# Expert matmuls in four column strips during attention, and the last 64 keys on the same tiles with zeros in V

## The chip, the cores and the metric

The kernel runs on one core of one Trainium2 chip. The core has a matrix engine (TensorE, PE in the profile, with its weight loads shown apart as PEld), a vector engine (VectorE, DVE), a scalar engine (ScalarE, ACT), a general engine (GpSimd, POOL), which here only starts loads, and SyncE (SP), which starts stores. Sixteen DMA engines move data between the chip's main memory and the on-chip memory. The metric is the time of one execution on the device, in microseconds (us); lower is better.

## What is computed

Attention of 8 batches, 12 heads, 448 tokens and 64 numbers a head, and behind it a feed-forward layer ("experts" below) on its 3,584 rows of 768:

```python
def _attn_ref(q, k, v):
    scale = 1.0 / np.sqrt(q.shape[-1])
    scores = scale * np.matmul(q, k.transpose(0, 1, 3, 2))
    scores = scores - np.max(scores, axis=-1, keepdims=True)
    attn = np.exp(scores)
    attn = attn / (np.sum(attn, axis=-1, keepdims=True) + 1e-09)
    return np.matmul(attn, v)

def _moe_ref(x, w_in, w_out):          # w_in 768 x 2048, w_out 2048 x 768
    h = x @ w_in
    g = h * (1.0 / (1.0 + np.exp(-h)))
    return g @ w_out
...
x = attn_out.transpose(0, 2, 1, 3).reshape(B * S, H * D)
return _moe_ref(x=x, **moe_kwargs)
```

## The kernel before

*Units.* Heads are taken four at a time, so a batch has three head groups. A unit is one head group of one batch; batch 0 is cut in two pieces of 224 tokens, so that it has six units of 224 and the other batches have three of 448, 27 units in all. The 448 keys of a group lie in four chunks (`c` = 0 to 3). In the first four groups ("lone") these chunks have 128, 128, 96 and 96 keys. From there on two groups go together, "low" and "high": each fills three chunks of 128 and has 64 keys left; the low group's are put in partitions 0 to 63 of the fourth chunk, the high group's in 64 to 127, so that both share one tile of exponentials, `E[(ns[0], 3)]`.

*Attention on PE.* Scores (L327) run on row tiles: a head's 64 numbers are folded to 32 partitions and two steps, so four matmuls on 32x128 tiles run together, one for each head. ACT takes the exponential (L364) into `E`. The row sums (`attend_sums`, L406) and the product with V (`attend_mm`, L390) run on column tiles: 128 keys by 32 columns, four heads together. For a pair the fourth chunk's product uses eight 64x32 tiles, four heads of each of the two groups. DVE inverts the sums and multiplies (L443 to L473), which leaves the rows of x, transposed, in `xT`.

*Experts on PE.* `ffn1` (L487) makes one 128-column piece of h from six matmuls on the full 128x128 array; ACT takes tanh and DVE the gate into `G`. The output product is done for four blocks at a time with seven products in place of eight (`product`, L685; `combine_g` and `combine_w` make the sums for it on DVE); two row blocks are done plainly (`plain`, L699). The last two batches use a seven-product form for h too (`pair_product`, L622), which runs when attention is over.

*Weights of a tile.* A matmul instruction on PE always stands behind its own weight load, so each matmul is two instructions in PE's order.

*The order.* It is written out beforehand: `Order` keeps a clock for each engine, every piece of work is an `Op` with an assumed cost, and in each round the main loop (from L1443) picks what PE does next: scores if they are due, else the products of attention that are ready, else an expert piece from the list `moe`. `on_pe` adds `SWITCH` = 0.094 to an Op whose mode (rows, columns, full, and the two "rest" modes) differs from the one ahead. Engines then run their instructions strictly in the order so made. POOL's order of loads is the order of the plan calls at L801 to L827: keys, queries and V of batch 0, the weights, then group by group; each load waits until its buffer is free.

*Buffers.* V of a batch lies in one tile of a ring of two, taken anew for each batch (L266); two of these tiles serve again at the end for sums of the weights (`old_buffer`, L555). Two chains of zero matmuls (L1438) fill PE's first microseconds, until the first experts run (`warm["on"]`).

*Lines that matter below.* Before the change L390 and L406 are attention's column tiles, L327 the row tiles, L487, L622, L685 and L699 the experts. In the changed file all experts are issued by one line.

Of the kernel before, what the change touches and what calls it, by code (L numbers as in the profile page):

```python
# [25 lines left out]
def mm(n):  # L26
    return n / 2400.0 + 0.0026
# [37 lines left out]
class Op:  # L65


    def __init__(self, eng, busy, emit, deps=(), bias=0.0, tail=HOP, then=None):
        self.eng, self.busy, self.emit = eng, busy, emit
        self.deps, self.bias, self.tail, self.then = list(deps), bias, tail, then  # L70
        self.done = None
        self.half = False

    def ready(self):
        return when(self.deps)
# [2 lines left out]
class Order:  # L78


    def __init__(self, shy):
        self.now, self.shy = 0.0, shy
        self.free = {"PE": 1.0, "ACT": 2.1, "DVE": 1.2, "POOL": 1.2}
        self.wait = {"ACT": [], "DVE": []}
        self.pool = []
        self.dma_free = 0.0
        self.out = []
        self.mode = None
        self.busy = {e: 0.0 for e in self.free}

    def add(self, op):
# [4 lines left out]
        self.out.append((self.now, len(self.out), fn))  # L96

    def start(self, op):
        self.emit(op.emit)
        self.free[op.eng] = self.now + op.busy  # L100
        self.busy[op.eng] += op.busy
        op.done = self.now + op.busy + op.tail
        if op.then:
            op.then(op.done)

    def on_pe(self, op, mode):
        gap = SWITCH if mode != self.mode else 0.0
        self.mode = mode
        op.busy += gap
        self.start(op)  # L110
# [55 lines left out]
def kernel(  # L166
# [69 lines left out]

    rawk, rawq, KT, QT, VT, E, T, acc, rdn_t, xT, g_t, ost_t = ({} for _ in range(12))
    sT_t, inv_t = {}, {}  # L240
    pS_t = {}

# [19 lines left out]


    def load_v(b, hg0, hg1, x):
        if b not in VT:
            VT[b] = sb.tile([128, NH, NCH, D], FP16, name=f"V_{b}", tag="V", bufs=2)  # L266
        hs = slice(HG * hg0, HG * hg1)
        first, count = X_TOK[form(b, hg0)][x]
        nc.gpsimd.dma_start(  # L269
            out=VT[b][32 * x : 32 * (x + 1), hs, 0:count, :],  # L270
            in_=v[b, hs].rearrange("h (i g) d -> i h g d", g=TPP)[
                :, :, first : first + count, :
            ],
        )
# [37 lines left out]
    def turn_q(n):  # L312
        t = rawq[n][:].bitcast(FP32).rearrange("p (g i) -> p g i", i=32)
        nc.vector.transpose(out=t, in_=t)  # L314
        QT[n] = rawq[n].rearrange("p (q e) -> p e q", e=2)

    def score_banks(n, w, ys):
        for y in ys:
# [63 lines left out]
    def attend_mm(a, n, part, c, h, k0, k1, e, start, stop):  # L382
        b, hg, g0, g1 = units[n]
        nq = 32 * (g1 - g0)
        at = nq * (c % per_burst(n))
        if part == 0:
            w = ones[k0:k1, :]
        else:
            w = VT[b][k0:k1, HG * hg + h, c, part - 1 :: 2]
        nc.tensor.matmul(  # L390
            out=a[32 * h : 32 * (h + 1), 0:nq],
            lhsT=w,
            rhs=e[k0:k1, h, at : at + nq],
            start=start,
            stop=stop,
        )
# [15 lines left out]
                )  # L412

    def attend(ns, part):
        made = []
        lone = len(ns) == 1
        if part == 0 and not lone:
            attend_sums(ns)
            return
        for n in ns:  # L420
            a = ps.tile([128, 512], FP32, name=f"a_{n}_{part}", tag="m", bufs=4)
            made.append(a)
            acc[(n, part)] = a
            for c in range(NCH if lone else NCH - 1):
                for h in range(HG):
                    attend_mm(
                        a, n, part, c, h, 0, rows_of(n, c), E[(n, c // per_burst(n))],
                        c == 0, lone and c == NCH - 1,
                    )
        if not lone:  # L430
            for h in range(HG):
                for i, n in enumerate(ns):
                    attend_mm(
                        made[i], n, part, 3, h, 64 * i, 64 * (i + 1), E[(ns[0], 3)],
                        False, True,
                    )

    def inverse(ns, step, i=0):
# [45 lines left out]
    def ffn1(b, f, t0, t1):  # L484
        h = ps.tile([128, 512], FP32, name=f"h_{b}_{f}_{t0}", tag="m", bufs=4)
        for cc in range(NDC):
            nc.tensor.matmul(  # L487
                out=h[:, 0 : t1 - t0],
                lhsT=w_in_t[:, cc, 128 * f : 128 * (f + 1)],
                rhs=x3(b, cc)[:, cc % 3, t0:t1],  # L490
                start=(cc == 0),
                stop=(cc == NDC - 1),
            )
        h_t[(b, f, t0)] = h
# [60 lines left out]
    def old_buffer(name, home, cols):  # L555

        if home == "V":
            t = sb.tile([128, NH, NCH, D], FP16, name=name, tag="V", bufs=2)
            t = t.rearrange("p h c d -> p (h c d)")
        else:  # L560
            t = sb.tile([128, HG, S], FP16, name=name, tag="E", bufs=NE)
            t = t.rearrange("p h s -> p (h s)")
        return [
            t[:, 3 * cols * i : 3 * cols * (i + 1)].rearrange("p (c t) -> p c t", c=3)
            for i in range(2 if home == "V" else 1)
        ]
# [36 lines left out]
    def pair_product(f, m):  # L603
        if m in (1, 5):
            pp_t[(f, PBANK[m])] = ps.tile(
                [128, 512], FP32, name=f"f_{f}_{m}", tag="m", bufs=4
            )[:, 0:S]
        elif m == 6:
            two = ps.tile([128, 2, 512], FP32, name=f"f_{f}_{m}", tag="s", bufs=2)
            pp_t[(f, "B")], pp_t[(f, "D")] = two[:, 0, 0:S], two[:, 1, 0:S]  # L610
        x = {(r, i): x3(PB + r, 3 * i) for r in range(2) for i in range(2)}
        lo, at = f // 4 * 4, slice(128 * (f % 4), 128 * (f % 4 + 1))
        a, w = {
            1: (x[0, 0], w_in_part(0, 0, f, f + 1)),
            2: (x[0, 1], w_in_part(1, 0, f, f + 1)),
            3: (sx_t.get(4), w_in_part(1, 1, f, f + 1)),
        }.get(m, (None, None))
        if a is None:
            i = {4: 4, 5: 1, 6: 2, 7: 3}[m]
            a, w = x[1, 1] if m == 4 else sx_t[i], tw_t[(i, lo)][:, :, at]  # L620
        for c in range(3):
            nc.tensor.matmul(  # L622
                out=pp_t[(f, PBANK[m])],
                lhsT=w[:, c, :],
                rhs=a[:, c, :],
                start=(c == 0 and m in (1, 6, 5)),
                stop=(c == 2),
                skip_group_check=True,
            )
# [45 lines left out]
    def product(qd, m):  # L675
        a, b = 2 * qd, 2 * qd + 1
        if m in (5, 6):
            w = S_t[(qd, m - 4)]
        else:
            t, i = {1: (a, 0), 2: (a, 1), 3: (a, 1), 7: (b, 0), 4: (b, 1)}[m]  # L680
            w = rows(t, i)
        if BANK[m] == m:
            pr_t[(qd, m)] = ps.tile([128, 512], FP32, name=f"p_{qd}_{m}", tag="m", bufs=4)
        for f in range(HF):
            nc.tensor.matmul(  # L685
                out=pr_t[(qd, BANK[m])][:, 0:OH],
                lhsT=w[:, f, :],
                rhs=W_[m][:, f, :],
                start=(f == 0 and BANK[m] == m),
                stop=(f == HF - 1),  # L690
                skip_group_check=True,
            )


    def plain(t, j, f0, f1):
        if f0 == 0:
            pr_t[("o", t, j)] = ps.tile([128, 512], FP32, name=f"o_{t}_{j}", tag="m", bufs=4)
        for f in range(f0, f1):
            nc.tensor.matmul(  # L699
                out=pr_t[("o", t, j)][:, 0:OH],  # L700
                lhsT=rows(t, f // HF)[:, f % HF, :],
                rhs=B_[f // HF, j][:, f % HF, :],
# [624 lines left out]
    def av_at():  # L1327
# [12 lines left out]
        for n in ns:  # L1340
            if len(exp_op.get(n, ())) < 2 * NCH // per_burst(n):
                return None
            first = 0.0 if n == ns[0] else (NCH - 1) * mm(S)
            for i, x in enumerate(exp_op[n]):
                c = i // 2 * per_burst(n)
                if len(ns) == 2 and c == NCH - 1:
                    c = 2 * (NCH - 1) - (n != ns[0]) * (NCH - 1)
                deps.append((x, first + c * mm(32 * (units[n][3] - units[n][2]))))
            if part:
                deps += [(x, LATE * (b == 0)) for x in ld_v[units[n][:2]]]  # L1350
# [9 lines left out]
    def run_av():  # L1360
# [6 lines left out]
            mms = 3 if two else 4  # L1367
        else:
            m_ring.take(len(ns))
            mms = 7 if two else 4  # L1370
        op = Op(
            "PE",
            mms * mm(nq) + 0.013 + (0.03 + SWITCH if two and part else 0.0),
            lambda: attend(ns, part),
            tail=PE_OUT,
        )
        if part == 2:

            def then(at):
                for _ in range(7 if two else NCH // per_burst(ns[0])):  # L1380
                    e_ring.give(at)
                if any(units[n][1] == NG - 1 and units[n][3] == TPP for n in ns):
                    v_ring.give(at)

            op.then = then
        elif part == 0 and two:
            op.then = lambda at: [t_ring.give(at) for _ in ns]
        od.on_pe(op, "cols")
        if two and part:
            od.mode = "rest cols"  # L1390
        if part == 0:
            after_sums(ns, op, nq)
        else:
# [49 lines left out]
    while True:  # L1443
        plan_turns(qk_seq[0][0][0] + 3 if qk_seq else NU)
        plan_adds()
        plan_pair()
        plan_sums()
        soon = od.step()
        if od.free["PE"] <= od.now:
            ran = False  # L1450
# [80 lines left out]
```

## Time and profile before

| | |
|---|---|
| runs | 395.69, 396.17, 396.07 us; median 396.07 |
| the profiled execution | 396.11 us |
| its span in the profile | 394.3 us |
| granted TensorE clock, mean over the span | 1.00 |
| instructions in the profile | 9,242 |
| exponentials (L364), ACT | 172, 149.9 us |
| ffn1 (L487), PE | 672 matmuls, 118.9 us |
| output products (L685), PE | 728 matmuls in several groups, the largest 368 with 65.3 us |
| scores (L327), PE | 864 matmuls, 56.7 us |
| product with V (L390), PE | 864 matmuls, 40.6 us |

Times are read from the profile of one execution. A matmul's own duration in it (for example 352 ns for 448 columns) is longer than the distance to the next one, since matmuls are pipelined; the distance between starts is what adds up to time. Four matmuls on separate tiles overlap, so a line with four times the matmuls need not take four times as long. "issue" as the releaser of an idle time means that the engine waited for nothing that the profile shows. The page's view in 40 slices has slices of 9.86 us.

### The profile page before, as it was taken

The numbers are of one execution on the slowest core, as the hardware profiler recorded it, in microseconds if no ns is written. First come the engines' busy times: TensorE is split into PE (matmuls) and PEld (weight loads), VectorE is DVE, ScalarE is ACT, GpSimd is POOL, SyncE is SP. The second block draws the span as 40 slices with busy tenths as digits, with TensorE's granted clock in tenths as the row PEclk, the third lists the DMA queues.
The fourth block names the chain that finished last, engine by engine and source line by source line (L and its number), as shares of the span: only waits on it lengthen the run. The fifth ranks groups of instructions, "written<-read, shape, count | busy, mean of one in ns | idle before, by whom it ended". The sixth has DMA issues, their size and how long they took to land.

```text
span 394.3 us, 9242 instructions
## 1 busy us (share of the span) xinstructions
PE 387.6 (98%) x3679; PEld 200.0 (51%) x3679; DVE 272.7 (69%) x570; ACT 253.6 (64%) x404; POOL 83.6 (21%) x153
## 2 busy tenths in 40 slices
PE   8999999999999999999999999999999999999995
PEld 7667764443444444554444444444444555555563
DVE  2466676999967588963698576896879945457332
ACT  4988885696871986753974759867685236763221
POOL 7532547215001532330006131600000000000000
PEclk9999999999999999999999999999999999999999
DMA  7999999919033946292016683711100130001343
GB/s 116 204 210 210 162 179 187 154 35 141 13 65 79 148 56 86 50 193 62 2 23 90 116 162 52 98 24 31 51 2 7 33 99 25 2 1 29 95 110 90
DMA packets 35579, 34.43 MB, mean 87 GB/s; under 512 B 11600, under 2 KB 34000, under 8 KB 35536
## 3 DMA queue, kind: packets, MB, share of 16 engines
q0 software_dynamic: 24784, 22.82, 38.7%
q1 hardware_dynamic: 9984, 10.24, 9.6%
q10 hardware_dynamic: 768, 0.79, 0.8%
q8 instruction: 29, 0.48, 0.5%
q14 instruction: 14, 0.11, 0.1%
HBM read 45.61 MB, written 11.01 MB: 144 GB/s over the span
## 4 chain that ended last, share of the span: by engine, by line
PE 91%; DVE 4%; ACT 1%; DMA 1%; issue 1%; ACTq 0%; POOL 0%; DVEq 0%; POOLq 0%
PE p L685 28%; PE h L487 28%; PE s L327 12%; PE a L390 10%; PE f L622 8%; PE o L699 3%; PE a L406 2%; DMA rq<-in_q_dram 1%; DVE tw L598 1%; ACT E L364 1%; PE z L1438 1%; DVE G L533 1%; ACTq L734 0%; DVE S L671 0%; DVE G L671 0%
## 5 line engine op out<-in xcount | busy, mean ns | idle before, releaser
L364 ACT ACTIVATE E<-s 128x896 f16<-128x896 f32 (+1 forms) x172 | 149.9, 915 | 22.6 <-PE s L327 21.2
L487 PE MATMUL h<-xT,w_in_t 128*128 128x448 f16 (+1 forms) x672 | 118.9, 327 | 0.0
L487 PEld LDWEIGHTS <-w_in_t 128*128 128x128 f16 x672 | 61.1, 98 | 54.4 <-issue 18.8
L498 ACT ACTIVATE th<-h 128x448 f16<-128x448 f32 (+1 forms) x112 | 54.3, 495 | 31.6 <-PE h L487 21.5
L533 DVE SCALAR_TENSOR_TENSOR G<-th,h 128x448 f16<-128x448 f16 (+2 forms) x112 | 55.1, 507 | 16.0 <-ACT th L498 14.0
L685 PE MATMUL p<-w_out_t,G 128*128 128x384 f16 x368 | 65.3, 326 | 0.3 <-DVE xT L473 0.2
L685 PEld LDWEIGHTS <-G 128*128 128x128 f16 x472 | 45.3, 98 | 33.4 <-issue 4.0
L269 POOL DMA_DIRECT2D V<-in_v_dram x88 | 48.6, 570 | 57.1 <-PE a L390 43.6
L327 PE MATMUL s<-rq,KT 32*128 32x448 f16 (+4 forms) x864 | 56.7, 340 | 0.6 <-ACT E L364 0.4
L742 ACT COPY ost<-p 128x384 f32<-128x384 f32 x39 | 18.7, 479 | 48.5 <-PE p L685 33.5
L390 PE MATMUL a<-E,V 128*32 128x448 f16 (+3 forms) x864 | 40.6, 335 | 0.0
L473 DVE SCALAR_TENSOR_TENSOR xT<-a,rdn 128x448 f16<-128x448 f32 (+1 forms) x54 | 28.9, 568 | 12.5 <-PE a L390 11.7
L254 POOL DMA_DIRECT2D rq<-in_q_dram x27 | 15.2, 561 | 105.2 <-PE s L327 85.8
L685 PE MATMUL p<-D,S 128*128 128x384 f16 x208 | 37.4, 327 | 0.0
L327 PEld LDWEIGHTS <-KT 32*128 32x128 f16 (+2 forms) x864 | 17.5, 98 | 28.7 <-issue 25.9
L390 PEld LDWEIGHTS <-V 128*32 128x32 f16 (+2 forms) x864 | 18.2, 95 | 22.6 <-issue 15.3
L375 DVE TENSOR_TENSOR T<-T,E 128x1792 f16<-128x1792 f16 x20 | 21.7, 1086 | 11.4 <-ACT E L364 11.4
L685 PEld LDWEIGHTS <-S 128*128 128x128 f16 x208 | 19.4, 98 | 16.2 <-issue 3.1
L375 DVE TENSOR_TENSOR T<-E,E 128x1792 f16<-128x1792 f16 x20 | 21.7, 1083 | 7.8 <-ACT E L364 7.8
L647 ACT ACTIVATE G<-f 128x448 f16<-128x448 f32 x32 | 16.2, 547 | 8.4 <-PE f L622 8.3
L304 DVE STREAM_TRANSPOSE KT<-rk 128x256 f32<-128x256 f32 (+3 forms) x48 | 16.6, 384 | 5.9 <-DMA rk<-in_k_dram 5.8
L314 DVE STREAM_TRANSPOSE rq<-rq 128x448 f32<-128x448 f32 (+1 forms) x27 | 15.3, 570 | 6.0 <-DMA rq<-in_q_dram 5.9
(124 smaller groups left out, 323.6 us busy)
## 6 DMA issues: line engine op xcount, KB each, us to landing
out_dram<-ost SPq DMA_DIRECT2D x208, 48.0 KB, 1.6
rk<-in_k_dram POOLq DMA_DIRECT2D x24, 224.0 KB, 4.9
rq<-in_q_dram POOLq DMA_DIRECT2D x21, 224.0 KB, 5.2
w_in_t<-in_moe_w_in_dram POOLq DMA_DIRECT2D x6, 512.0 KB, 11.6
w_out_t<-in_moe_w_out_dram POOLq DMA_DIRECT2D x4, 768.0 KB, 12.9
V<-in_v_dram POOLq DMA_DIRECT2D x43, 64.0 KB, 3.8
V<-in_v_dram POOLq DMA_DIRECT2D x40, 48.0 KB, 3.6
out_dram<-ost ACTq DMA_DIRECT2D x16, 48.0 KB, 1.8
```

The source lines that it names most:

```text
L269: nc.gpsimd.dma_start(out=VT[b][32 * x : 32 * (x + 1), hs, 0:count, :], in_=v[b, hs].rearrange("h (i g) d -> i h g d", g=TPP)[:, :, first ...
L327: nc.tensor.matmul(out=pS[p0 : p0 + 32 * (x1 - x0), h % 2, at : at + nq], lhsT=KT[(b, hg)][32 * h : 32 * (h + 1), c, x0:x1, :, e], rhs=QT[ ...
L364: nc.scalar.activation(out=E[(n, w)][0:kr, 2 * y : 2 * y + 2, 0:nk], in_=pS_t[(n, w, y)][0:kr, :, 0:nk], func=AF.Exp, scale=attn_scale,)
L375: nc.vector.tensor_tensor(out=T[n], in0=T[n] if step else E[(n, 0)], in1=E[(n, step + 1)], op=ALU.add,)
L390: nc.tensor.matmul(out=a[32 * h : 32 * (h + 1), 0:nq], lhsT=w, rhs=e[k0:k1, h, at : at + nq], start=start, stop=stop,)
L473: nc.vector.scalar_tensor_tensor(out=x3(b, cc)[:, cc % 3, 32 * g0 : 32 * g1], in0=acc[(n, part)][:, 0:nq], scalar=0.5, in1=rdn_t[n].rearra ...
L487: nc.tensor.matmul(out=h[:, 0 : t1 - t0], lhsT=w_in_t[:, cc, 128 * f : 128 * (f + 1)], rhs=x3(b, cc)[:, cc % 3, t0:t1], start=(cc == 0), s ...
L498: nc.scalar.activation(out=th, in_=h_t[(b, f, t0)][:, 0 : t1 - t0], func=AF.Tanh)
L533: nc.vector.scalar_tensor_tensor(out=dst[:, f, at + lo : at + hi], in0=th_t[(b, f, t0)][:, lo - t0 : hi - t0], scalar=1.0, in1=h_t[(b, f, ...
L622: nc.tensor.matmul(out=pp_t[(f, PBANK[m])], lhsT=w[:, c, :], rhs=a[:, c, :], start=(c == 0 and m in (1, 6, 5)), stop=(c == 2), skip_group_ ...
L685: nc.tensor.matmul(out=pr_t[(qd, BANK[m])][:, 0:OH], lhsT=w[:, f, :], rhs=W_[m][:, f, :], start=(f == 0 and BANK[m] == m), stop=(f == HF - 1),
L742: nc.scalar.copy(out=ost(qd, i, j), in_=bank(qd, m))
```

## The change

Three things are changed.

1. While attention lasts, an expert matmul of 128x128 is issued as four matmuls of 128x32, each with its own weight load of 32 columns, its own 32 partitions of the output, and the same moving data (`wide`, which replaces `nc.tensor.matmul` in `ffn1`, `pair_product`, `product` and `plain`). `Order.on_pe` then calls the mode "cols". "While attention lasts" is from the first experts (the six matmuls that end the warm-up stay whole) until neither scores nor products of attention are left.
2. For a pair, the fourth chunk's product with V is done like the others, on 128x32 tiles with all 128 keys of the shared tile `E[(ns[0], 3)]`, once for each of the two groups. The 64 rows of V that belong to the other group hold zeros. The planner's costs go from 7 to 8 matmul steps for a pair.
3. V lies in two fixed tiles used in turn. Six `memset`s on DVE write the zeros: two at the start (the second tile, groups 1 and 2), and after the last use of batch 0 three for the first tile and after batch 1 one for the second. The loads of V fill only the other rows, so that the zeros stay.

```diff
@@ class Order
+        self.strips = False
+        self.attention = True
...
     def start(self, op):
-        self.emit(op.emit)
+        self.emit(lambda: self.run(op))
...
+    def run(self, op):
+        self.strips = op.strips
+        op.emit()
+
     def on_pe(self, op, mode):
+        if mode == "full" and self.attention:
+            mode, op.strips = "cols", True
         gap = SWITCH if mode != self.mode else 0.0
...
+    VT = [const.tile([128, NH, NCH, D], FP16, name=f"V{i}") for i in range(2)]
+
+    def clear_v(i, hg, low):
+        rows = slice(64, 128) if low else slice(0, 64)
+        nc.vector.memset(VT[i][rows, HG * hg : HG * (hg + 1), NCH - 1], 0.0)
+
+    for hg in (1, 2):
+        clear_v(1, hg, hg == 1)
...
     def load_v(b, hg0, hg1, x):
-        if b not in VT:
-            VT[b] = sb.tile([128, NH, NCH, D], FP16, name=f"V_{b}", tag="V", bufs=2)
...
+    def wide(out, lhsT, rhs, **flags):
+        n = 4 if od.strips else 1
+        for j in range(n):
+            at = slice(128 // n * j, 128 // n * (j + 1))
+            nc.tensor.matmul(out=out[at], lhsT=lhsT[:, at], rhs=rhs, **flags)
...
     def attend(ns, part):
...
-            for c in range(NCH if lone else NCH - 1):
+            for c in range(NCH):
+                e = E[(ns[0] if c == NCH - 1 else n, c // per_burst(n))]
                 for h in range(HG):
                     attend_mm(
-                        a, n, part, c, h, 0, rows_of(n, c), E[(n, c // per_burst(n))],
-                        c == 0, lone and c == NCH - 1,
-                    )
-        if not lone:
-            for h in range(HG):
-                for i, n in enumerate(ns):
-                    attend_mm(
-                        made[i], n, part, 3, h, 64 * i, 64 * (i + 1), E[(ns[0], 3)],
-                        False, True,
+                        a, n, part, c, h, 0, rows_of(n, c), e, c == 0, c == NCH - 1
                     )
...
     def ffn1(b, f, t0, t1):
         h = ps.tile([128, 512], FP32, name=f"h_{b}_{f}_{t0}", tag="m", bufs=4)
         for cc in range(NDC):
-            nc.tensor.matmul(
+            wide(
...
     def old_buffer(name, home, cols):
         if home == "V":
-            t = sb.tile([128, NH, NCH, D], FP16, name=name, tag="V", bufs=2)
-            t = t.rearrange("p h c d -> p (h c d)")
+            t = VT[name[:2] == "sx"].rearrange("p h c d -> p (h c d)")
...
     def run_av():
...
-            mms = 7 if two else 4
+            mms = 8 if two else 4
         op = Op(
             "PE",
-            mms * mm(nq) + 0.013 + (0.03 + SWITCH if two and part else 0.0),
+            mms * mm(nq) + 0.013,
...
                 if any(units[n][1] == NG - 1 and units[n][3] == TPP for n in ns):
                     v_ring.give(at)
+                    i = units[ns[-1]][0]
+                    for hg in range(NG if i == 0 else 1 if i == 1 else 0):
+                        low = i == 0 and hg != 1
+                        od.add(
+                            Op("DVE", 0.2, lambda hg=hg, low=low: clear_v(i, hg, low), [op], 5)
+                        )
...
         od.on_pe(op, "cols")
-        if two and part:
-            od.mode = "rest cols"
...
         plan_sums()
+        od.attention = bool(qk_seq or av_seq) and not warm["on"]
         soon = od.step()
```

More of the change, by code (lines that the diff above doesn't have):

```diff
@@ L88, in __init__ @@
         self.mode = None
+        self.strips = False
+        self.attention = True
         self.busy = {e: 0.0 for e in self.free}
@@ L233 @@
     w_out_t = const.tile([128, NFF, DM], FP16, name="w_out_t")
-    rawk, rawq, KT, QT, VT, E, T, acc, rdn_t, xT, g_t, ost_t = ({} for _ in range(12))
+    VT = [const.tile([128, NH, NCH, D], FP16, name=f"V{i}") for i in range(2)]
[4 more added lines that the diff above has]
+        clear_v(1, hg, hg == 1)
+    rawk, rawq, KT, QT, E, T, acc, rdn_t, xT, g_t, ost_t = ({} for _ in range(11))
     sT_t, inv_t = {}, {}
@@ L269, in load_v @@
         nc.gpsimd.dma_start(
-            out=VT[b][32 * x : 32 * (x + 1), hs, 0:count, :],
+            out=VT[b % 2][32 * x : 32 * (x + 1), hs, 0:count, :],
             in_=v[b, hs].rearrange("h (i g) d -> i h g d", g=TPP)[
@@ L388, in attend_mm @@
         else:
-            w = VT[b][k0:k1, HG * hg + h, c, part - 1 :: 2]
+            w = VT[b % 2][k0:k1, HG * hg + h, c, part - 1 :: 2]
         nc.tensor.matmul(
@@ L414, in attend @@
     def attend(ns, part):
-        made = []
         lone = len(ns) == 1
@@ L421, in attend @@
             a = ps.tile([128, 512], FP32, name=f"a_{n}_{part}", tag="m", bufs=4)
-            made.append(a)
             acc[(n, part)] = a
-            for c in range(NCH if lone else NCH - 1):
+            for c in range(NCH):
+                e = E[(ns[0] if c == NCH - 1 else n, c // per_burst(n))]
                 for h in range(HG):
                     attend_mm(
-                        a, n, part, c, h, 0, rows_of(n, c), E[(n, c // per_burst(n))],
-                        c == 0, lone and c == NCH - 1,
-                    )
-        if not lone:
-            for h in range(HG):
-                for i, n in enumerate(ns):
-                    attend_mm(
-                        made[i], n, part, 3, h, 64 * i, 64 * (i + 1), E[(ns[0], 3)],
-                        False, True,
+                        a, n, part, c, h, 0, rows_of(n, c), e, c == 0, c == NCH - 1
                     )
@@ L621, in pair_product @@
         for c in range(3):
-            nc.tensor.matmul(
+            wide(
                 out=pp_t[(f, PBANK[m])],
@@ L684, in product @@
         for f in range(HF):
-            nc.tensor.matmul(
+            wide(
                 out=pr_t[(qd, BANK[m])][:, 0:OH],
@@ L698, in plain @@
         for f in range(f0, f1):
-            nc.tensor.matmul(
+            wide(
                 out=pr_t[("o", t, j)][:, 0:OH],
@@ L1342, in av_at @@
                 return None
-            first = 0.0 if n == ns[0] else (NCH - 1) * mm(S)
+            first = 0.0 if n == ns[0] else NCH * mm(S)
             for i, x in enumerate(exp_op[n]):
                 c = i // 2 * per_burst(n)
-                if len(ns) == 2 and c == NCH - 1:
-                    c = 2 * (NCH - 1) - (n != ns[0]) * (NCH - 1)
                 deps.append((x, first + c * mm(32 * (units[n][3] - units[n][2]))))
```

## The prediction

> **What bounds the kernel now.** I read the page first, then the order of time on TensorE (PE), then PE's waits, then the DMA queues by stage.
>
> ```profile
> PE 387.6 (98%) x3679; PEld 200.0 (51%) x3679; DVE 272.7 (69%) x570; ACT 253.6 (64%) x404; POOL 83.6 (21%) x153
> DMA  7999999919033946292016683711100130001343
> q8 instruction: 29, 0.48, 0.5%
> PE 91%; DVE 4%; ACT 1%; DMA 1%; issue 1%; ACTq 0%; POOL 0%; DVEq 0%; POOLq 0%
> ```
>
> PE carries 91% of the chain that ended last, so the time moves with PE's own time. The DMA engines are full (nines) from 10 to 79 us. The third line is PE's own code arriving: 29 packets, 0.48 MB. PE has 7,407 instructions (3,679 matmuls, as many weight loads, 49 others), so one takes 64 bytes and one packet brings 256.
>
> ```profile
> 153.94 0.58 PE L327 MATMUL s<-rq,KT 32*128 32x448 f16 x8
> 154.44 1.31 PE L487 MATMUL h<-xT,w_in_t 128*128 128x448 f16 x6
> 155.59 1.46 PE L685 MATMUL p<-w_out_t,X 128*128 128x384 f16 x8
> 170.49 0.56 PE L406 MATMUL a<-T,half 128*32 128x448 f16 x8
> 170.88 0.36 PE L406 MATMUL a<-E,both 128*32 128x448 f16 x4
> ```
>
> Here I read steps and switches (columns: start, us, what, count). In the records behind these rows, full matmuls of 448 columns start 0.189 us apart, those of 384 columns 0.162. Four matmuls on four 128x32 strips start together, and the next four 0.189 later (170.688, 170.877): four strips take the time of one full matmul. Where the tile shape changes, the next start is late: 153.650 to 153.935 is 0.285, so 0.096 over a step.
>
> ```profile
> 27.39 0.56 PE L390 MATMUL a<-E,ones 128*32 128x224 f16 x13
> 28.43 0.28 PE L390 MATMUL a<-E,ones 96*32 96x224 f16 x3 [0.49 <-issue]
> 28.43 0.10 PEld L390 LDWEIGHTS <-ones 96*32 96x32 f16 x3 [0.75 <-issue]
> DMA  9999999999999999999998999999999999999999
> q8 instruction: 1, 0.02, 1.2%
> rq<-in_q_dram POOLq DMA_DIRECT2D x1, 224.0 KB, 16.4
> ```
>
> The first three rows are PE's timeline, the last three the DMA view of 28.4 to 33.1. PE halts between the first and second strip of one step, at its instruction 962, for 0.75 us. No instruction there waits for a semaphore, and the releaser is "issue". I read it as PE out of code. A code packet ran from 26.02 to 26.97; PE went on 1.46 later. One packet's worth of instructions earlier, weight load 707, the last of four that otherwise start 3 ns apart, comes 66 ns late, at 22.21: 1.41 after the packet that ended at 20.80. The next packets begin 3.8 and 3.7 us behind these two points (26.02, 32.12). So with the DMA engines full a refill takes 3.7 + 0.95 + 1.44 = 6.1 us from edge to edge, and the packets of this stage do begin 6.0 to 6.2 apart (19.85, 26.02, 32.12, 38.08). That is 24 ns an instruction, which the kernel touches already.
>
> **The change, part by part.** The sum is made against the profiled execution: span 394.3, its time 396.11, so 1.8 lies around the span; the median of the runs is 396.07.
>
> *Switches.* From the two built programs, counted by tile shape in PE's order, with mean costs from the records: full to columns 14 becomes 1 (0.093 each), columns to full 12 becomes 3 (0.106), columns to 64x32 20 becomes 0 (0.103), 64x32 to full 14 becomes 0 (0.127), to columns 5 becomes 0 (0.124), to rows 1 becomes 0 (0.127). That is 1.2 + 1.0 + 2.1 + 1.8 + 0.6 + 0.1 = 6.8 us removed. Switches to and from the row tiles of the scores stay, 173 before and 174 after; some 60 of them now leave columns (0.104) and not full (0.096), 49 enter columns (0.103) and not full (0.107): +0.4 with the one more. Net -6.4.
>
> *The last 64 keys.* Before, one step of eight 64x32 matmuls served both head groups; now each has a step of its own: 20 steps more, 20 x 0.189 = +3.8. The 64 zero rows cost no more than that.
>
> *Strips on the array.* 1,138 expert matmuls become 4,552. The nearest rows are the strips of attention: over 123 such steps of 448 columns the excess over 0.189 is 0.4 us in all. From below 0; from above, if every step kept the stagger of a first one (four starts over 0.010 us), 1,138 x 0.010 = 11.4. I take 0, since the attention rows are the same tiles.
>
> [...]
>
> *Code.* PE's instructions rise from 7,407 to 14,236, and the order of jobs on PE around batch 0's experts is the same in both programs. From the first of these to the last (30.06 to 58.13, 28.1 us) PE has 721 instructions before and 1,837 after. The edges where new code is needed lie 256 apart in PE's order, behind 962 at 1218, 1474 and so on to 2754, the seventh; the stage ends at 2886. If refills never bind the cost is 0, as all of it hides under the matmuls. If each takes 6.1 us, the seventh edge is passed at 28.43 + 42.7 = 71.1, and the last 132 instructions, at 28.1 / 1,837 = 0.015 each, end at 73.1: +15.0. Between the ends: the DMA engines are full in this stage but for about 46 to 51 us. A prompt refill takes at least 1.0 + 0.95 + 1.44 = 3.4 us (the packet at 44.97 began 1.0 after PE was 40 instructions short of its edge, the later ones 1.1 in the mean) and at most 6.1; I take 4.5, since how far ahead of execution code is asked for isn't shown. Five refills at 6.1 and two at 4.5 end the stage at 28.4 + 39.5 + 2.0 = 69.9: **+11.8**. Next, to the first of batch 1's experts (75.64), 765 instructions, 3.0 refills, 18.2 us against 17.5: +0.7. From there to the end of attention (305.1) there are 9,603, 37.5 refills in 229.4 us, 6.1 us for each: not binding at 4.5. Products are tightest, 144 instructions in 3.2 us, 5.7 a refill; at 6.1, some 19 of them would give 0.4 each, 7.6. Taken as 0.
>
> What a halt makes late: behind PE stand the scores, so ACT's exponentials and DVE's sums of them; both have idle time in this stage (of each 8 us between 38 and 62, ACT is busy 6.3 to 6.9, DVE 4.6 to 6.3), so the halt is paid once, by PE.
>
> *V and its zeros.* Six memsets on DVE, at 0.07 to 0.11 us (its memsets at the start): two before the first keys land, four beside PE's experts; 0.4 us if the cover were gone. Behind one on DVE stands a normalization that the next experts need, so at most 0.1 late each. On POOL the loads of V for batches 2 and 3 wait for them, and the next keys and queries stand behind; POOL's present waits there are for PE itself (43.6 us in all for V), so this adds nothing.
>
> Sum: 394.3 - 6.4 + 3.8 + 11.8 + 0.7 = 404.2, and 1.8 around it: **406.0 us**.
>
> **The rivals.**
>
> *Code keeps up (the other side).* If more code is held ahead than these halts suggest, or refills come faster when asked for sooner, the experts of batch 0 cost nothing and the rest stands: 394.3 - 2.6 + 1.8 = 393.5, faster. It decides at 28.1 / 1,837 x 256 = 3.9 us a refill. For it: after 100 us most packets begin early and PE never halts without a waiter. Against: the halt at 28.43 and the late load at 22.21, both 1.4 us behind a packet. [...] By that rule the time is this rival's, 393.5; the two late edges show otherwise, so it gets 0.13.
>
> *Refills bind everywhere.* If 6.1 us is the refill's own time, whatever the DMA engines do: 15.0 + 0.7 + 7.6 = 23.3, and 394.3 - 2.6 + 23.3 + 1.8 = 416.8. For it: in the calm slices a packet lands 1.0 us after its start as in the full ones, so only the delay before it differs. Against: most later packets start nearer to their place. 0.18.
>
> *Half the refills are prompt.* PE runs longer while the loads stay the same, so the DMA engines empty sooner against PE: 3.5 x 6.1 + 3.5 x 4.5 = 37.1, +9.4 for the stage, and with prompt ones at 3.4 it is 33.3, +5.6: 399.8 to 403.6. The lower part, 396 to 399, gets 0.06; the rest is in the likeliest's own range.
>
> *Strips cost on the array.* [...] 0.03.
>
> **How the numbers follow.** The likeliest, code late while the loads run, has 0.60 with a range of its own of 399 to 411. Code keeping up 0.13, near 393.5; the light case 0.06, 396 to 399; refills bound everywhere 0.18, 411 to 420; strips 0.03. The range 397 to 418 leaves out the first rival, and the ends of the light case and of the tails above, together about 0.2. About 0.2% (0.8 us) is what this kernel's runs can tell from no change. Faster is 0.13, same 0.03 (the lowest part of the light case), slower 0.84.
>
> **What would show it.** PE's code queue with some 55 packets and 0.9 MB; PE and its weight loads idle for "issue" at strips that wait for nothing, in batch 0's experts, at code edges some 6 us apart; that stage about 40 us long and not 28; steps of 0.189 within strips; the stretch after attention as before (89 us). Wrong: no such idle time, or a shorter stage (code kept up); idle time of that kind in the products after 100 us (bound everywhere); strip steps over 0.195.

## The result, and the profile after

| | before | changed |
|---|---|---|
| median of the runs | 395.88 us (395.56 to 396.17) | 407.62 us (405.03 to 409.78) |
| the profiled execution, its span | 396.11, 394.3 us | 407.56, 405.5 us |
| ratio, 95% interval | | 1.029, 1.026 to 1.032 |
| granted clock, mean | 1.00 | 0.99 |

The change makes the kernel slower by 11.7 us; 406.0 was predicted, with a range of 397 to 418. One run without strips (414.11 us, a mean clock of 0.949) and one with the strips alone (417.24 us, 0.955) are slow ones and left out of their kernels' medians and ratios below.

The page of the changed kernel: busy time, three rows of the 40 slices (10.14 us each now), PE's code queue, and the chain that ended last.

```profile
PE 389.0 (96%) x7093; PEld 214.9 (53%) x7093; DVE 274.0 (68%) x576; ACT 253.5 (63%) x404; POOL 83.6 (21%) x153
PE   8996787999999999999999999999999999999995
PEclk9999898999999999999999999999999999999999
DMA  8999999290906616358227176260200031000343
q8 instruction: 55, 0.90, 0.9%
PE 92%; issue 3%; DVE 2%; DMA 1%; ACT 1%; ACTq 0%; DVEq 0%; POOLq 0%
```

PE's busy time has hardly grown (387.6 to 389.0), while the span is 11.2 longer: the time is lost where PE does nothing. The PE row places it: the fourth to seventh slices, 30 to 71 us, are no longer nines, and behind them nothing has changed. In the same slices the DMA row is all nines. The chain has 3% "issue" where it had 1%, and code packets went from 29 to 55.

PE's waits and, below, its timeline (start, us, what, count, idle time before and its releaser) show the halts. A row of the waits gives us in total, how often, and the longest.

```profile
PE h L337 <- issue: 5.5, 3, 2.2
PE s L349 <- issue: 4.0, 2, 2.6
```

```profile
32.12 0.74 PE L337 MATMUL h<-xT,w_in_t 128*32 128x224 f16 x22
34.08 0.85 PE L337 MATMUL h<-xT,w_in_t 128*32 128x224 f16 x26 [1.23 <-issue]
...
35.37 2.48 PE L337 MATMUL h<-xT,w_in_t 128*32 128x224 f16 x94
40.01 0.85 PE L337 MATMUL h<-xT,w_in_t 128*32 128x224 f16 x26 [2.16 <-issue]
...
60.19 0.57 PE L349 MATMUL s<-rq,KT 32*128 32x448 f16 x6
63.37 0.56 PE L349 MATMUL s<-rq,KT 32*128 32x448 f16 x2 [2.61 <-issue]
```

The first halt parts 22 strips from the next 26 of one run of experts, the last comes between the sixth and seventh of eight score matmuls. Nothing in the program stops PE at such places, and no instruction there waits for a semaphore. Counted in PE's order the five halts come right before instructions 1218, 1474, 1730, 2242 and 2498, five of the seven edges that the prediction listed. Each time PE goes on 1.28 to 1.38 us after the end of a code packet (32.79, 38.70, 44.55, 55.61 and 62.09).

### The profile page after: what moved, and what is told of

The parts are those of the page before. It is cut to its first block, busy times and chain, and to the rows that moved or that the text cites. A ratio compares the mean times of both kernels' runs of the same rounds, so it can differ in the third digit from the quotient of the medians.

```text
span 405.5 us, 16083 instructions
## 1 busy us (share of the span) xinstructions
PE 389.0 (96%) x7093; PEld 214.9 (53%) x7093; DVE 274.0 (68%) x576; ACT 253.5 (63%) x404; POOL 83.6 (21%) x153
## 3 DMA queue, kind: packets, MB, share of 16 engines
q1 hardware_dynamic: 9984, 10.24, 9.3%
## 4 chain that ended last, share of the span: by engine, by line
PE 92%; issue 3%; DVE 2%; DMA 1%; ACT 1%; ACTq 0%; DVEq 0%; POOLq 0%
PE h L337 29%; PE p L337 28%; PE s L349 12%; PE a L412 10%; PE f L337 8%; PE o L337 3%; PE a L428 2%; DMA rk<-in_k_dram 1%; PE z L1452 1%; DVE p L758 1%; DVE tw L610 0%; ACTq L746 0%; DVE T L397 0%; ACT ost L754 0%; ACT E L386 0%
## 5 line engine op out<-in xcount | busy, mean ns | idle before, releaser
L337 PE MATMUL h<-xT,w_in_t 128*32 128x448 f16 (+2 forms) x2670 | 121.3, 329 | 5.5 <-issue 5.5
L337 PEld LDWEIGHTS <-w_in_t 128*32 128x32 f16 (+1 forms) x2742 | 73.9, 98 | 63.1 <-issue 22.3
L337 PEld LDWEIGHTS <-G 128*32 128x32 f16 (+1 forms) x1544 | 55.0, 97 | 35.7 <-issue 4.8
L337 PE MATMUL p<-w_out_t,G 128*32 128x384 f16 (+1 forms) x1016 | 65.5, 326 | 0.7 <-DVE xT L486 0.4
L349 PE MATMUL s<-rq,KT 32*128 32x448 f16 (+4 forms) x864 | 57.6, 342 | 4.9 <-issue 4.0
L412 PE MATMUL a<-E,V 128*32 128x448 f16 (+2 forms) x864 | 42.5, 340 | 0.0
L486 DVE SCALAR_TENSOR_TENSOR xT<-a,rdn 128x448 f16<-128x448 f32 (+1 forms) x54 | 29.2, 564 | 13.0 <-PE a L412 11.8
L337 PE MATMUL p<-D,S 128*32 128x384 f16 (+1 forms) x544 | 37.5, 327 | 0.0
L412 PEld LDWEIGHTS <-V 128*32 128x32 f16 (+1 forms) x864 | 21.8, 98 | 17.0 <-issue 4.8
L337 PEld LDWEIGHTS <-S 128*32 128x32 f16 (+1 forms) x544 | 20.7, 97 | 14.9 <-issue 2.7
L337 PE MATMUL p<-D,G 128*32 128x384 f16 (+1 forms) x272 | 19.1, 326 | 0.0
```

What stands on the lines that cost most here:

```text
L337: nc.tensor.matmul(out=out[at], lhsT=lhsT[:, at], rhs=rhs, **flags)
L349: nc.tensor.matmul(out=pS[p0 : p0 + 32 * (x1 - x0), h % 2, at : at + nq], lhsT=KT[(b, hg)][32 * h : 32 * (h + 1), c, x0:x1, :, e], rhs=QT[ ...
L412: nc.tensor.matmul(out=a[32 * h : 32 * (h + 1), 0:nq], lhsT=w, rhs=e[k0:k1, h, at : at + nq], start=start, stop=stop,)
L486: nc.vector.scalar_tensor_tensor(out=x3(b, cc)[:, cc % 3, 32 * g0 : 32 * g1], in0=acc[(n, part)][:, 0:nq], scalar=0.5, in1=rdn_t[n].rearra ...
```

## The experiments

Theory: PE runs out of code while batch 0's experts are strips and the loads fill the DMA engines; everything else in the change is worth some 2 us of gain. Rivals: the strips cost something on the array; the 64 keys or the fixed V tiles cost it; refills take 6 us everywhere.

**The change without strips** (all else kept):

```diff
-        od.attention = bool(qk_seq or av_seq) and not warm["on"]
+        od.attention = False
```

> Experts whole all through; V in two fixed tiles, zeros and the eight-step pairs kept. Theory (halts for code, caused by the strips' instructions alone): PE's order has 7,407 instructions as before, so no halts. Against before 20 steps more (+3.8 us), 20 column to 64x32 switches and the ones out of 64x32 go, 14 column to full switches come (-3.0): +0.8, span 395.1, ratio 1.002. Rival (the zeros in V, the fixed tiles or the longer pairs delay loads and cost most of the loss): +8 us or more, ratio 1.02.

Measured: 396.73 us, ratio 1.0018 (1.0008 to 1.0027). The keys and V's two tiles cost 0.7 us and not 8: they are not where the time went.

**The strips alone** (keys and V as before): the kernel before with `wide`, `Order.run` and the "cols" mode of `on_pe`.

> Experts in strips while attention lasts, but the last 64 keys on 64x32 tiles and V's ring as before. Theory: batch 0's experts have the same 1,837 instructions, so the same halts (10.3 us in the changed kernel's profile) and the half clock behind the long ones (3.4); switches -1.9: span about 406, ratio 1.03. Rival (V's part costs): no more than +1 us over before, ratio 1.00.

Measured: 407.99 us, ratio 1.0298 (1.0279 to 1.0317), the whole loss. PE halts before the same five instructions, 1218, 1474, 1730, 2242 and 2498. By tile and shape PE's matmuls are the same ones in both kernels until far behind these places (the first 1,713), so this run does not tell the instruction count from the job that stands there. A run below does, in which the order of PE's jobs differs (the zeros written in small pieces): it halts at 962, 1218 and 1474 all the same.

**Batch 0's first products whole**, the rest of the change kept, and the same with the plain products whole too:

```diff
-    def on_pe(self, op, mode):
-        if mode == "full" and self.attention:
+    def on_pe(self, op, mode, whole=False):
+        if mode == "full" and self.attention and not whole:
...
-                od.on_pe(op, "full")
+                od.on_pe(op, "full", b == 0)
```

> As the changed kernel, but batch 0's experts whole; 13,120 instructions on PE, 721 in batch 0's experts as before. Theory: no halt in batch 0, at most one short one (under 1 us) in the plain products behind it, clock full; -2.4 from switches and steps: span 392 to 393, ratio 0.996 (0.994 to 0.998). Rival (a strip costs by itself, anywhere): 3,808 of 4,552 strips are left, so 0.84 of the loss: span 403.7, ratio 1.024. Rival (refills bind everywhere): +7 in the products, ratio 1.015.

> As the last, with the plain products behind batch 0 whole too; 12,735 instructions. Theory: the refills up to 75 us are as in before, so no halt at all; 205 switches and not 201 (+0.4): span 392 to 393, ratio 0.995 (0.993 to 0.998). If the plain products' strips did halt in the run before, this is faster than it by that halt; if not, 0.4 slower. Rivals as there: ratio 1.02 and 1.015.

Measured: 394.09 us (393.92 to 394.43), ratio 0.995 (0.9937 to 0.9962), and 394.6 us, 0.9962 (0.995 to 0.9975). The first beats both kernels. Its page:

```profile
PE 385.3 (98%) x6535; PEld 213.6 (54%) x6535; DVE 273.9 (70%) x576; ACT 253.2 (65%) x404; POOL 83.6 (21%) x153
PEclk9999999999999999999999999999999999999999
DMA  8999999909067145293090390711100130001333
q8 instruction: 51, 0.84, 0.8%
```

6,535 of the 7,093 matmuls are left, 51 of 55 packets still come, the clock is whole, and no "issue" is left in PE's waits. 558 matmuls moved the time by 13.5 us, by where they stood. Strips as such cost next to nothing: without batch 0's the change gains the 2 us that fewer switches were to give. The plain products as strips had not halted, so making them whole gave only switches back (0.5 us).

**Dense code without load.** Is 256 instructions in 6 us the refill's own pace? In the kernel of 394.09 us the matmuls of batch 3's first products, which run where the DMA engines have less to do (a share of 0.22 to 0.32 from 180 to 200 us), were cut in two of 224 columns, then in four of 112 (the diff), which puts 3,545 instructions into that stretch.

```diff
+        cut = [(t0, t1)] if b != 3 else [(t0 + 112 * i, t0 + 112 * (i + 1)) for i in range(4)]
-        for cc in range(NDC):
-            wide(out=h[:, 0 : t1 - t0], ..., rhs=x3(b, cc)[:, cc % 3, t0:t1], ...)
+        for c0, c1 in cut:
+            for cc in range(NDC):
+                wide(out=h[:, c0 - t0 : c1 - t0], ..., rhs=x3(b, cc)[:, cc % 3, c0:c1], ...)
```

> Run e3, with each expert matmul of batch 3 (about 200 to 230 us, where the loads are light) cut in two of 224 tokens: from its first expert to its last 2,009 instructions on PE in place of 1,241, in some 27 us of matmuls, 3.4 us for 256. Theory, with a refill of 3.4 us where the loads are light (the one prompt refill seen in the changed kernel, from the edge passed at 45.93, was that fast): just not binding, 0 to +1 us over e3, 394 to 395. If such a refill takes 4.5 us: +4 to +5. Rival (6.1 us always): 48 us for this stretch, +20.

> As e5, but cut in four of 112 tokens: 3,545 instructions in the stretch, 13.8 refills, under 2 us of matmuls for 256. Theory: halts at each edge 256 apart although the loads are light; at 3.4 us a refill +17 to +20 over e3 (about 411 to 414), and the distance of the edges measures the refill. At 4.5 us +30; at 6.1 us +55. Rival (it is not code; short strips wait for their weight loads): no halts at edges, but longer steps throughout; or +1 us if neither binds.

Measured, one execution of each: 394.9 us without a halt in that stretch, where 256 instructions now take about 3.5 us or more, and 417.81 us, 23.7 more in the span than the uncut kernel. PE's timeline of the second:

```profile
190.91 0.70 PE L337 MATMUL h<-xT,w_in_t 128*32 128x112 f16 x41 [1.53 <-issue]
...
194.36 1.58 PE L337 MATMUL h<-xT,w_in_t 128*32 128x112 f16 x113 [1.15 <-issue]
...
197.82 1.76 PE L337 MATMUL h<-xT,w_in_t 128*32 128x112 f16 x128 [1.15 <-issue]
201.27 0.90 PE L337 MATMUL h<-xT,w_in_t 128*32 128x112 f16 x57 [1.70 <-issue]
```

These four halts are 256 instructions and 3.45 us apart (3.45, 3.46, 3.45): with the engines calm (a DMA share of 0.02 from 190.91 to 201.27) a refill takes 3.45 us from edge to edge, 1.1 to the packet's start, about 0.95 for the packet, 1.4 until PE goes on. The next two edges, as calm, are 3.73 apart, with packets of 1.05 and 1.15 us. In the first stage of the changed kernel it was 5.93 (34.08 to 40.01), with 3.65 to the packet's start. So dense enough code halts PE in a calm stretch too, and 6 us is a matter of the load. The loss lies above the 17 to 20 that go with 3.4 us, and below the 30 that go with 4.5: two edges beside a late packet are 4.0 and 5.9 apart, and 10.24 us of half clock follow the halts, up to 5 us of loss that no theory had.

Of the halts over 0.25 us eleven stand in this stretch, all at such edges and none between them, so the short strips do not wait for their weight loads. A twelfth, of 0.5 us, stands at 123.78, at an edge among products that the uncut kernel passes without a halt: products, too, can lie near the bound.

**The same strips with less to load**, in three kernels, since two moved more than the load. All leave 3/4 of w_out unloaded, 2.4 MB.

First with the rows set to zero by one large `memset` at the start:

```diff
+    nc.vector.memset(w_out_t[:, NFF // 4 :], 0.0)
...
-    plan_w_out(NFF // 4, NFF // 2)
...
-    plan_w_out(NFF // 2, 3 * NFF // 4)
-    plan_w_out(3 * NFF // 4, NFF)
```

> The changed kernel, but three quarters of w_out are never loaded: they are zeros from a memset on DVE at the start (so the output leaves out those rows' part). The code and the matmuls of batch 0's experts stay (1,821 instructions). 4.7 MB less to read, some 22 us of full DMA engines. Theory (refills are late because the DMA engines are full): the two halts behind 50 us (1.6 and 2.7 us) and the second stretch at half clock (1.7) go, the first three halts stay: -4 to -7 us against the changed kernel, ratio to before 1.012 to 1.020. Rival (a refill takes 6.1 us by itself): as the changed kernel, ratio 1.029.

Measured: 413.29 us, ratio 1.0435 (1.0409 to 1.0461), a miss. The page and a window (from:to, us, then busy us and count of PE, its loads, DVE, ACT and POOL, granted clock, DMA share, GB/s; the share is the packets' time over that of 16 engines and can pass 1, 1.09 here):

```profile
PEclk9555599999999999999999999999999999999999
```

```profile
8.00:50.00 42.00, 41.73 (x530) 24.34 (x526) 14.21 (x40) 23.58 (x27) 16.61 (x29) 0.51 1.09 171
```

The `memset` held DVE at the start, PE's scores waited 2.0 us for DVE's queries, up to 7.84, and the clock was half for 40.96 us from 8.70 on. PE was busy all the time, but on 530 matmuls where the changed kernel has 873 in the same window, and so it asked for code more slowly; behind that stretch two edges alone held it, by 0.3 us each. In this execution the loss goes with the clock; of loads and refills its time tells nothing. That the clock is the whole cause isn't shown: the fourth run of this kernel took 413.56 us at a mean clock of 0.998, and where it lost its time isn't known.

Then in small pieces, from the landing of the first part of w_in on (the three loads removed as above):

```diff
+    for f0 in range(NFF // 4, NFF, 2):
+        wout_rows.append(f0)
+        ld_wout.append(
+            od.add(
+                Op(
+                    "DVE",
+                    1.3,
+                    lambda f0=f0: nc.vector.memset(w_out_t[:, f0 : f0 + 2], 0.0),
+                    [ld_win[0][0]],
+                    25,
+                )
+            )
+        )
```

> The changed kernel, but of w_out only the first quarter of its rows is loaded; the other three quarters are set to zero by DVE in pieces of two rows, from the landing of the first part of w_in on, and the products with them give zeros. So 3/4 of that load is gone from the DMA queues while batch 0's experts run, and PE's instructions stay as they are (14,236 in all, within ten). The pieces are spread this time, so that PE is not held at the start and keeps its clock. Theory (a refill is late because the DMA engines are full, and prompt otherwise, 3.5 us): the first three halts lie before the loads would have ended anyhow and partly stay, the two behind 50 us (1.6 and 2.7 us) and the second stretch of half clock (1.7) go: 4 to 7 us less than the changed kernel, a ratio to the kernel before of 1.012 to 1.020. Rival (a refill takes 6 us from edge to edge in this stage whatever the DMA engines do): halts at the same edges and the same ratio as the changed kernel, 1.026 to 1.032. Third way: should the pieces on DVE hold the normalizations that the experts wait for, PE's idle time would be put down to DVE and not to issue, and the time is then read by the halts alone.

Measured: 410.67 us, ratio 1.038 (1.0353 to 1.0407), outside both, and the third way of the expectation. PE's waits:

```profile
PE h L337 <- issue: 4.6, 2, 2.7
PE s L349 <- ACT E L386: 3.0, 5, 1.0
PE s L349 <- DVE rq L330: 2.3, 2, 1.4
PE a L412 <- issue: 1.1, 1, 1.1
```

By the halts alone it goes with the theory: those at 962, 1218 and 1474 are there, and no edge behind 41 us halts, where the changed kernel has three more. But the pieces put the order of jobs out, and PE now waits for DVE's queries and ACT's exponentials (5.3 us, against 0.8 in the changed kernel), with two windows of half clock beside them. Such waits give the packets time as well, so this run alone doesn't settle it.

Last with nothing on DVE and every job in its place: each load brings one row of four, and what uses the other three reads that row. PE's matmuls are the same ones in the same order as in the changed kernel.

```diff
-            out=w_out_t[:, f0:f1],
-            in_=moe_w_out[128 * f0 : 128 * f1]...
+            out=w_out_t[:, f0 : f0 + 1],
+            in_=moe_w_out[128 * f0 : 128 * f0 + 128]...
...
-                rhs=W_[m][:, f, :],
+                rhs=W_[m][:, f // 4 * 4 if m in (1, 2, 3) else f, :],
...
-                rhs=B_[f // HF, j][:, f % HF, :],
+                rhs=B_[f // HF, j][:, f % HF // 4 * 4, :],
```

> The changed kernel, but each of the four loads of w_out brings the first of its four rows of 128 alone, and every use of the others reads that row instead (the products are then not the reference's). The loads keep their number and their places in the queues, PE's instructions and the order of jobs are those of the changed kernel, nothing is set to zero on DVE; 2.4 MB of 3.1 are gone, some 11 us of full DMA engines (0.2 MB per us in these slices), in two lots: half behind 24 us, half behind 49. Theory (a refill is late because the DMA engines are full, and prompt otherwise): the halt at edge 1218 stays, that at 1474 stays or shrinks, those at 1730, 2242 and 2498 (2.3, 1.6 and 2.7 us) shrink or go, and the second stretch of half clock with them: 5 to 9 us less than the changed kernel, span 396 to 401, a ratio to the kernel before of 1.006 to 1.018. Rival (a refill takes 6 us in this stage whatever the DMA engines do): the same five halts, ratio 1.026 to 1.032.

Measured: 402.54 us (401.43 to 404.66), ratio 1.0169 (1.013 to 1.0208), span 400.2: 5.3 less than the changed kernel, at the slow end of what the theory gave and away from the rival's. Its waits, and its last halts in the timeline:

```profile
PE h L337 <- issue: 3.4, 2, 2.2
PE s L349 <- issue: 1.9, 2, 1.0
```

```profile
50.81 0.37 PE L349 MATMUL s<-rq,KT 32*128 32x448 f16 x2 [0.93 <-issue]
...
55.64 0.37 PE L349 MATMUL s<-rq,KT 32*128 32x448 f16 x2 [0.96 <-issue]
```

The first two halts, while the engines are still full, are as before (1218 at 34.42, 1474 at 40.34, 5.92 apart). Edges 1730 and 2498, worth 2.3 and 2.7 us, pass without one, 1986 and 2242 halt for about 1.1 each, and one stretch of half clock is left of two. The same window, first here, then in the changed kernel:

```profile
60.00:70.00 10.00, 9.97 (x276) 6.36 (x272) 5.81 (x11) 7.94 (x14) 0.00 (x0) 1.00 0.02 5
```

```profile
60.00:70.00 10.00, 7.39 (x172) 4.12 (x166) 4.38 (x11) 4.76 (x10) 3.28 (x6) 0.83 1.05 154
```

With a DMA share of 0.02 PE is busy 9.97 of 10 us on 276 matmuls, with 1.05 it is busy 7.39 on 172. The two windows don't hold quite the same part of the order, and half clock lies in the second, so the same edge in both kernels says it better. Behind edge 2242 the packet started 4.24 us late in the changed kernel (56.90 to 61.14, a DMA share of 1.15 in between) and 1.10 us late here (55.64 to 56.74, a share of 0.00). Over the edges 1218 to 2498 of the changed kernel, the one with strips alone and this one, eighteen in all, the five with a share up to 0.91 before the packet's start had it 1.04 to 1.28 us behind the edge, and the thirteen with 1.04 and more 1.60 to 4.24. So full DMA engines make the refill late; what in the engines delays the packet's start, and not the packet, isn't shown.

## Why the prediction was right

| term | predicted, us | measured, us |
|---|---|---|
| switches | -6.4 | together -2.1 (span of the kernel with batch 0 whole, against 394.3) |
| the last 64 keys | +3.8 | (in the line above; -2.6 predicted for both) |
| strips on the array | 0 | 0.4 over 433 steps of 448 columns (against 0.189), 0.4 over 432 of 384 (against 0.162) |
| code, batch 0's experts | +11.8 | halts 10.3, half clock 3.4 |
| code, up to batch 1's experts | +0.7 | no halt |
| span | 404.2 | 405.5 |

*Switches and keys.* Right, to half a microsecond in the sum. The two weren't parted on the array, but without strips, where fewer switches go, the rest of the change cost 0.7 us.

*Strips.* Right: steps of four strips go at the pace of one whole matmul, 0.189 us for 448 columns and 0.163 for 384 in the median, with the strips' weight loads, 97 to 98 ns each in the mean, inside them.

*Code.* The place, the edges and the pace were right: from 962 on the edges are passed at 28.14, 34.08, 40.01, 45.93, 51.62, 56.90, 63.37 and 69.33, which is 5.3 to 6.5 apart, and the last group of batch 0's experts starts at 70.80 where it started at 57.63 (changed, then before):

```profile
70.80 0.76 PE L337 MATMUL h<-xT,w_in_t 128*32 128x224 f16 x24
```

```profile
57.63 0.75 PE L487 MATMUL h<-xT,w_in_t 128*128 128x224 f16 x6
```

Two sizes were off, in opposite directions. A prompt refill takes 3.45 us, near the lower bound of 3.4, and not the 4.5 taken; and a term was missing, the clock. That the sum came within 1.3 us of the span is luck in part, since the two nearly cancel. The halts themselves cost 10.3 us (each idle distance less one step: 1.4, 2.3, 2.3, 1.6 and 2.7), less than the 12.5 predicted, since edges 1986 and 2754 passed without one: the packets for them started 1.04 and 1.89 us behind 1730 and 2498. Before both edges PE ran at half clock, 46.09 to 49.51 and 63.16 to 66.57, and each stretch costs about half of its 3.41 us: in the first, steps of four strips of 224 columns start 0.187 us apart, at 42.0 us, with the full clock, 0.096. That hardly stands in the place of a halt: 1.3 us behind its packet the code for the two edges was there at about 49.3 and 67.7, and 1.7 us earlier PE would have come to them at 49.9 and 67.6. The measured sum, -2.1 + 10.3 + 3.4 = 11.6, comes near the 11.2 by which the span grew.

*What stands behind the halts.* It was said that ACT and DVE lose nothing further: the stretch from the end of attention to the end of the span is 89.2 us (316.3 to 405.5), 88.9 before, and PE's waits for ACT and DVE stay below 0.5 us each but for the first, 1.0, at the start. Nothing on PE waits for the new memsets.

*The rivals.* Code keeping up fell with the five halts; its time, 393.5, is nearly that of the kernel with batch 0 whole (394.09), where code does keep up. Refills bound everywhere fell too: not one halt of the changed kernel lies behind 64 us, products included, and calm refills take 3.45. The light case asked for prompt refills at half of the edges; in this stage only the packet behind 1730 started promptly (1.04 us), the others 1.9 to 4.2 us behind their edges. No run shows a rule that would have put the changed kernel on the side of code keeping up: PE stood for 10.3 us there, at edges 256 instructions apart.

## What to carry to other kernels

A matmul cut into four strips was free on the array here but is four times the code: count PE's instructions over each stretch, and where 256 of them (matmuls and weight loads) take less than about 3.5 us, or 6 us while loads fill the DMA engines, expect PE to stop for code as it did here (3.45 and 5.93 us a refill), and no wait in the program will say so. Look for "issue" as the releaser between two alike matmuls, and at the spacing of those places in instructions. The gain of such a change can be kept by leaving it out where the loads run: here with 558 matmuls fewer it goes from 2.9% slower to 0.5% faster.

## What the runs showed of the hardware that was not expected

The clock fell to half behind windows in which PE was still busy for 1.28 and 1.01 of 3.41 us. In the changed kernel the record of the clock begins at 5.13 and changes at 46.09, 49.51, 63.16 and 66.57, which are 40.96, 3.41, 13.65 and 3.41 apart: 12, 1, 4 and 1 times the shortest, which is 3.413 in the trace. So its windows can be read on that grid (columns as above):

```profile
35.85:39.27 3.42, 2.00 (x82) 1.74 (x75) 1.22 (x4) 2.16 (x5) 0.54 (x1) 1.00 1.15 209
...
42.68:46.09 3.41, 1.28 (x48) 0.95 (x37) 1.09 (x4) 1.20 (x3) 1.08 (x2) 1.00 1.22 182
46.09:49.51 3.42, 3.42 (x66) 2.40 (x68) 0.78 (x2) 1.63 (x3) 3.13 (x6) 0.50 0.80 85
...
59.75:63.16 3.41, 1.01 (x30) 0.37 (x19) 1.76 (x5) 1.51 (x3) 0.55 (x1) 1.00 1.25 201
63.16:66.57 3.41, 3.20 (x34) 1.18 (x33) 0.98 (x2) 0.92 (x1) 2.64 (x5) 0.50 1.06 155
```

After a window in which PE was busy 1.28 or 1.01 us the next is granted half; after one with 2.00 it is not. So a halt of the same length costs 1.7 us more or not, by how it lies on the grid: the halt of 2.4 us before 40.01 is shared by two windows, that before 45.93 is not. With the strips alone windows of 1.25 and 0.92 us are followed by half clock, in the last kernel with less to load one of 1.25, in the kernel with batch 3 cut in four those of 1.44 and 1.21, while 1.80 and more is followed by the full clock there. The kernel with the small pieces does not fit a bound on busy time (1.38 is followed by the full clock, 2.12 by half), so the rule isn't settled. Half clock begins at 46.09 us in the changed kernel, at 40.24 with the strips alone and at 40.94 in the last kernel, 5.85 and 5.15 earlier, which are no whole steps of 3.413: the grid lies otherwise in these three executions. That the runs of the changed kernel spread over 4.7 us, and those of the kernel with batch 0 whole over 0.5, would go with a grid that lies otherwise in each run, but that is a guess: the fastest, 405.03 us, has the highest mean clock, 0.996 against 0.990 to 0.992; it was not followed up.

A code packet took 0.97 us with the DMA engines full (31.82 to 32.79), hardly more than the 0.95 of the calm stretch; its start was what came late, 3.65 us behind the edge and not 1.1.
